# A gated linear-attention block with a squared-ReLU layer: units of 64 tokens of two batches, on quarters of the array

## The chip, the core and the metric

The kernel runs on one core of a Trainium2 chip, as one launch. The core has a matrix engine (TensorE, PE in the rows; its weight loads are listed as PEld), a vector engine (VectorE, DVE), a scalar engine (ScalarE, ACT), GpSimd (POOL) and a sync engine (SP) from which most transfers are issued. Each engine works through its own list of instructions in order. The metric is the device time of one execution in microseconds; lower is better.

## What is computed

Four batches, eight heads, 768 tokens, 48 channels a head, all in float32. For each batch and head a 48x48 state is carried from token to token; its output is reshaped to 384 channels and goes through a second layer that mixes each token with the one before it:

```
cur   = (u * k_t) v_t^T
y_t   = r_t (state + cur)
state = w * state + k_t v_t^T

xk = mu_k * x + (1 - mu_k) * x_prev          (x: y of all heads, 384 wide)
xr = mu_r * x + (1 - mu_r) * x_prev
out = sigmoid(xr @ w_r) * (relu(xk @ w_k)^2 @ w_v)     (d_ff = 1024)
```

The term with `u` is called the bonus: it only weighs a token's own key and value.

## The kernel before

**Attention.** The recurrence is done in chunks: 128 tokens of one batch, all eight heads, six chunks a batch, 24 in all, walked batch by batch. `load` brings r and k with channels on the partitions (48 channels of an even head on partitions 0 to 47, of an odd head on 64 to 111), and from the ninth chunk on also r and k with tokens on the partitions (`nat`). `prepare` multiplies r and k with tables of powers of the decay (L206, VectorE) and builds the bonus: for the first eight chunks with small matmuls and transposes (L215, L221), later on GpSimd (L231, L232) with a VectorE reduction (L234); ScalarE then writes it on the diagonal of a 128x128 block per head (L240). `scores` (L250) multiplies keys with receptances, 128x128 tokens a head, and VectorE copies the causal part over the diagonal block (L253). `update` (L283) adds keys times values to the state, `outputs` multiplies state with receptance (L302) and values with scores (L307) into one accumulator, and `turn` (L323) copies the result to `xt`, whose last 16 rows of each half are filled by transfers (L329).

**Feed-forward.** A tile is 512 tokens in a row of one batch (or the end of one and the start of the next). `mix` makes the two mixtures, each split in a high and a low part; `ffn` does 8 blocks of keys, 3 of gates and 3 of values. Every product is three matmuls of 512 columns (high x high, high x low, low x high; L341): 72 + 27 + 72 = 171 a tile, 1026 in all. The weights arrive as 64-bit numbers in ten blocks, and each is turned into a high and a low part by ScalarE and VectorE (`split_weights`, L188 to L197: an absolute value, a clamp, a shift, two joins, a cast and a difference).

**Order.** Four chunks run ahead of the first tile. After that one step of the attention generator is put between feed-forward groups at a higher priority, and a scheduler settles the order on each engine. Idle matmuls (L98) fill the start.

The lines that the prediction touches: L206 (scaling), L240 and L253 (diagonal and mask), L229 to L234 (GpSimd's part), L250, L302, L307 and L283 (attention matmuls), L341 (feed-forward), L188 to L197 (weights).

Of the kernel before, what the change touches and what calls it, by code (L numbers as in the profile page):

```python
# [8 lines left out]
F32 = mybir.dt.float32  # L9
# [7 lines left out]
P = 128  # L17
B, H, S, D = 4, 8, 768, 48
C = 128
NC = S // C  # L20
# [9 lines left out]
TT = 512  # L30
TC = TT // C
NM = B * S // TT
# [5 lines left out]
BUSY, BUSY_LATER, BUSY_UPDATE, BUSY_COLS = 48, 24, 8, 192  # L38


AHEAD, PACE, URGENT = 4, 1.3, 1000

EARLY = 8

W_MIN, W_MAX = 0.75, 1.25

LEAST = 1.125 * 2.0 ** -15
G = P // (B * H)
# [3 lines left out]

def first_run(m):

    return min(TT, S - m * TT % S)


def runs(m, x):

    n = first_run(m)  # L60
    if n == TT:
        return x[:, 1:TT + 1], x[:, :TT]
    assert 2 * n == TT
    x = x[:, :TT + 2].rearrange("p (a n) -> p a n", a=2)
    return x[:, :, 1:], x[:, :, :n]
# [10 lines left out]
def rwkv_kernel(ctx, tc, rkT, nat, w_pair, u, u_pair, mu, r_seq, k_seq, v_seq, w_rep, u_rep, wk, wv, wr, out):  # L76
# [3 lines left out]
    inp = main.enter_context(tc.tile_pool(name="inp", bufs=2))  # L80
    att = main.enter_context(tc.tile_pool(name="att", bufs=2))
    xp = main.enter_context(tc.tile_pool(name="xp", bufs=2))
    moe = main.enter_context(tc.tile_pool(name="moe", bufs=2))
    stage = main.enter_context(tc.tile_pool(name="stage", bufs=2))
    psA = main.enter_context(tc.tile_pool(name="psA", bufs=2, space=bass.MemoryType.PSUM))
    psY = main.enter_context(tc.tile_pool(name="psY", bufs=3, space=bass.MemoryType.PSUM))
    psM = main.enter_context(tc.tile_pool(name="psM", bufs=3, space=bass.MemoryType.PSUM))

    idle = const.tile([P, BUSY_COLS], BF16, name="idle")
    nc.vector.memset(idle, 0.0)
    idle_ps = psM.tile([P, BUSY_COLS], F32, tag="m", name="idle_ps")

    def stay_busy(n, behind=None):
        with tc.issue_after(behind.ins) if behind else ExitStack():
            for _ in range(n):
                nc.tensor.matmul(out=idle_ps, lhsT=idle[:, :P], rhs=idle, start=True, stop=True, skip_group_check=True)  # L98

    stay_busy(BUSY)  # L100

    w_sb = const.tile([DR, NP], F32, name="w_sb")
    nc.sync.dma_start(out=w_sb, in_=w_pair)
    tiles = {}
    order = [(b, c) for b in range(B) for c in range(NC)]

    def load(b, c):
        rk = inp.tile([DR, 2, NP, C], F32, tag="rk", name=f"rk_{b}_{c}")  # L110
        nc.sync.dma_start(out=rk, in_=rkT[b, c])
        na = None
        if order.index((b, c)) >= EARLY:
            na = stage.tile([P, 2, DM], F32, tag="raw", bufs=2, name=f"nat_{b}_{c}")
            nc.sync.dma_start(out=na, in_=nat[b, c, :, :2])
        v = inp.tile([P, DM], F32, tag="v", bufs=3, name=f"v_{b}_{c}")
        nc.sync.dma_start(out=v, in_=nat[b, c, :, 2])
        tiles[b, c] = rk, na, v

    load(0, 0)  # L120
    u_sb = const.tile([DR, NP, 2], F32, name="u_sb")
    nc.sync.dma_start(out=u_sb, in_=u_pair)
    ident = const.tile([P, P], F32, name="ident")
    make_identity(nc, ident)
    causal_f = const.tile([P, C], F32, name="causal_f")
    nc.gpsimd.memset(causal_f, 1.0)
    nc.gpsimd.affine_select(out=causal_f, in_=causal_f, compare_op=ALU.is_gt, fill=0.0,
                            base=0, pattern=[[1, C]], channel_multiplier=-1)
    causal = causal_f.bitcast(U32)
    S_t = []  # L130
    for i in range(2):
        t = const.tile([DR, NP, HB], F32, name=f"S_{i}")
        nc.gpsimd.memset(t, 0.0)
        S_t.append(t)

    w_in = const.tile([DR, NP], F32, name="w_in")
    nc.vector.tensor_scalar(out=w_in, in0=w_sb, scalar1=W_MIN, scalar2=W_MAX, op0=ALU.max, op1=ALU.min)
    zero = const.tile([DR, 1], F32, name="zero")
    nc.vector.memset(zero, 0.0)
    zero = zero.broadcast_to([DR, C])  # L140

    table = const.tile([DR, 2, NP, C + 1], F32, name="table")
    pw, ipw = table[:, 0], table[:, 1, :, :C]
    nc.vector.memset(pw[:, :, 0:1], 1.0)
    for p in range(NP):
        nc.vector.tensor_tensor_scan(
            out=pw[:, p, 1:], data0=w_in[:, p:p + 1].broadcast_to([DR, C]), data1=zero,
            initial=1.0, op0=ALU.mult, op1=ALU.add)
    last_inv = const.tile([DR, NP, 1], F32, name="last_inv")
    nc.vector.reciprocal(out=last_inv, in_=pw[:, :, C:])  # L150
    nc.vector.tensor_tensor(out=ipw, in0=pw[:, :, C - 1::-1], in1=last_inv.broadcast_to([DR, NP, C]), op=ALU.mult)
    mu_sb = const.tile([P, 2, CT], F32, name="mu_sb")
# [442 lines left out]
```

## Time and profile before

| | |
|---|---|
| median of 2 runs | 406.65 us (405.02 and 408.28) |
| profiled execution, first to last instruction (span) | 408.4 us |
| TensorE busy | 394.9 us, 97% of the span |
| VectorE, ScalarE, GpSimd busy | 219.0, 235.6, 69.4 us |
| mean granted TensorE clock | 0.914 of full speed |
| last matmul ends, span ends | 401.9 us, 408.4 us |

One execution is profiled. Busy time adds up the durations of an engine's instructions where they do not overlap; a matmul that waits in the pipeline counts as busy, so TensorE at 97% is not TensorE at its peak. The chain of waits starts at the last instruction and follows back what released each step. The granted clock has two levels here, 1.2 and 2.4 GHz, given as 0.50 and 1.00; a figure between them is a mean over a stretch. A float32 matmul of the program appears as two TensorE instructions, so counts of attention matmuls in the rows are twice those of the program; the feed-forward ones appear once.

### The profile page before, as it was taken

To read this page: it belongs to the slowest core of one execution; us is meant where nothing else is said; L and a number is where in the kernel's file an instruction comes from. 1 tells how busy PE (TensorE), PEld (TensorE's weight loads), DVE (VectorE), ACT (ScalarE), POOL (GpSimd) and SP (SyncE) were. 2 spreads that over 40 slices of the span, in tenths; PEclk is the share of its full clock that TensorE was granted. 3 is DMA by queue.
4 is the path that set the end of the run, shared out by engine and by line. 5 is a ranking of instruction groups with operands and counts; after the bars stand their busy time and mean duration, and the time that the engine had idled before them with its cause. 6 is when DMAs were issued, how large, how long until landed. Compare 5 with 4: busy or idle time off the path is not lost.

```text
span 408.4 us, 6780 instructions
## 1 busy us (share of the span) xinstructions
PE 394.9 (97%) x2660; PEld 319.7 (78%) x2660; DVE 219.0 (54%) x338; ACT 235.6 (58%) x489; POOL 69.4 (17%) x66
## 2 busy tenths in 40 slices
PE   8999979998999999999999999999999999999993
PEld 7888867886678877677878887878888888888882
DVE  6569959986365854436782467641255136213110
ACT  3644647769855549764660988750894189128400
POOL 1000000068064503234630181000000000000000
PEclk9555985579999999997799999999999999999999
DMA  7646575432166131244442430001000100010001
GB/s 226 192 137 201 142 221 151 153 121 79 39 169 182 45 124 58 85 126 136 130 130 69 130 119 24 2 28 46 26 2 26 51 2 0 26 54 0 2 35 50
DMA packets 15463, 36.11 MB, mean 88 GB/s; under 512 B 2560, under 2 KB 7296, under 8 KB 15424
## 3 DMA queue, kind: packets, MB, share of 16 engines
q1 hardware_dynamic: 15424, 35.60, 28.3%
q8 instruction: 23, 0.38, 0.4%
q14 instruction: 16, 0.13, 0.1%
HBM read 29.70 MB, written 4.72 MB: 84 GB/s over the span
## 4 chain that ended last, share of the span: by engine, by line
PE 85%; DMA 4%; POOL 3%; DVE 3%; ACT 2%; issue 1%; POOLq 0%; DVEq 0%; ACTq 0%; SPq 0%
PE v L341 25%; PE k L341 22%; PE r L341 10%; PE a L250 9%; PE y L307 6%; PE y L302 6%; PE kt_ps L215 2%; DMA raw_v<-in_wv 2%; DMA nat<-in_nat 2%; PE idle_ps L98 2%; PE u L283 1%; POOL ku L231 1%; PE kt_ps L221 1%; ACT am L240 1%; PE u L273 1%
## 5 line engine op out<-in xcount | busy, mean ns | idle before, releaser
L372 ACT ACTIVATE kr<-k 128x512 f32<-128x512 f32 x48 | 28.5, 597 | 61.1 <-PE k L341 56.3
L377 DVE TENSOR_TENSOR kl<-kr,kh 128x512 fp32r<-128x512 f32 x48 | 35.1, 733 | 50.1 <-ACT kh L375 49.8
L341 PE MATMUL k<-xh,wk_hi 128*128 128x512 f32 x144 | 57.9, 405 | 1.4 <-ACT kr L372 1.4
L341 PE MATMUL k<-xl,wk_hi 128*128 128x512 f32 x144 | 57.2, 397 | 0.0
L341 PE MATMUL v<-kl,wv_hi 128*128 128x512 f32 x144 | 56.8, 395 | 0.0
L341 PE MATMUL v<-kh,wv_lo 128*128 128x512 f32 x144 | 56.6, 393 | 0.0
L341 PE MATMUL k<-xh,wk_lo 128*128 128x512 f32 x144 | 56.5, 392 | 0.0
L341 PE MATMUL v<-kh,wv_hi 128*128 128x512 f32 x144 | 56.4, 392 | 0.0
L240 ACT ACTIVATE am<-ident,dg 128x128 f32<-128x128 f32 x128 | 39.9, 390 | 24.2 <-PE y L307 13.4
L250 PEld LDWEIGHTS a<-RK 48*128 48x128 f32 x384 | 39.3, 221 | 9.5 <-issue 7.3
L250 PE MATMUL a<-RK 48*128 48x128 f32 x384 | 46.6, 323 | 0.0
L253 DVE COPY_PREDICATED am<-causal_f,a 128x512 f32<-128x512 uint32 x48 | 34.1, 730 | 18.9 <-PE a L250 13.7
L391 DVE TENSOR_TENSOR sg<-v,sg 128x512 f32<-128x512 f32 x18 | 12.4, 689 | 58.8 <-PE v L341 58.8
L231 POOL TENSOR_TENSOR ku<-nat,u_bc 128x384 f32<-128x384 f32 x16 | 24.3, 1516 | 106.6 <-DMA nat<-in_nat 98.0
L206 DVE TENSOR_TENSOR RK<-rk,table 112x1024 f32<-112x1024 f32 x24 | 30.2, 1256 | 13.6 <-PE y L302 9.0
L307 PE MATMUL y<-am,v 128*48 128x128 f32 x384 | 36.2, 319 | 0.4 <-DVE am L253 0.3
L302 PE MATMUL y<-RK,S 48*48 48x128 f32 (+1 forms) x320 | 32.1, 311 | 2.8 <-ACT kt L224 2.8
L341 PEld LDWEIGHTS k<-xh,wk_hi 128*128 128x128 f32 x144 | 27.3, 190 | 8.7 <-ACT kr L372 1.8
L341 PEld LDWEIGHTS v<-kh,wv_lo 128*128 128x128 f32 x144 | 27.0, 188 | 6.5 <-issue 0.4
L341 PEld LDWEIGHTS k<-xh,wk_lo 128*128 128x128 f32 x144 | 27.2, 189 | 6.1 <-issue 0.2
L341 PEld LDWEIGHTS v<-kh,wv_hi 128*128 128x128 f32 x144 | 27.0, 188 | 6.0
L341 PEld LDWEIGHTS v<-kl,wv_hi 128*128 128x128 f32 x144 | 27.1, 188 | 5.8
(94 smaller groups left out, 612.7 us busy)
## 6 DMA issues: line engine op xcount, KB each, us to landing
rk<-in_rkT SPq DMA_DIRECT2D x24, 448.0 KB, 4.0
nat<-in_nat SPq DMA_DIRECT2D x16, 384.0 KB, 3.3
v<-in_nat SPq DMA_DIRECT2D x24, 192.0 KB, 3.7
raw_k<-in_wk SPq DMA_DIRECT2D x4, 768.0 KB, 5.8
raw_v<-in_wv SPq DMA_DIRECT2D x4, 768.0 KB, 4.3
out<-sg SPq DMA_DIRECT2D x12, 256.0 KB, 2.0
out<-sg SPq DMA_DIRECT2D x12, 128.0 KB, 1.8
raw_r<-in_wr SPq DMA_DIRECT2D x2, 576.0 KB, 3.7
```

Source lines behind the costliest of these rows:

```text
L98: nc.tensor.matmul(out=idle_ps, lhsT=idle[:, :P], rhs=idle, start=True, stop=True, skip_group_check=True)
L206: nc.vector.tensor_tensor(out=RK, in0=rk, in1=table[:, :, :, :C], op=ALU.mult)
L231: nc.gpsimd.tensor_tensor(out=ku, in0=na[:, 1], in1=u_bc, op=ALU.mult)
L240: nc.scalar.mul(out=am[:, p], in_=ident, mul=dg[:, 2 * p + s:2 * p + s + 1])
L250: mm = nc.tensor.matmul(out=a_ps[s][:, p, :], lhsT=K[rows, p, :], rhs=R[rows, p, :], start=True, stop=True, skip_group_check=True)
L253: nc.vector.copy_predicated(out=Am[s], mask=causal.unsqueeze(1).broadcast_to([P, NP, C]), data=a_ps[s])
L302: nc.tensor.matmul(out=y_ps[s * HB:s * HB + n, p, :], lhsT=state[b, c][rows, p, :n], rhs=R[rows, p, :], start=(p == 0), stop=False, skip_g ...
L307: nc.tensor.matmul(out=y_ps[s * HB:s * HB + D, p, :], lhsT=v[:, h * D:(h + 1) * D], rhs=Am[s][:, p, :], start=(c == 0 and p == 0), stop=(p ...
L341: nc.tensor.matmul(out=ps, lhsT=a, rhs=x, start=(i == 0), stop=(i == n - 1))
L372: nc.scalar.activation(out=kr, in_=k_ps, func=AF.Relu)
L377: nc.vector.tensor_tensor(out=kl, in0=kr, in1=kh.bitcast(F32), op=ALU.subtract)
L391: nc.vector.tensor_tensor(out=sg[o], in0=v_ps, in1=sg[o], op=ALU.mult)
```

## The change

**Units.** A unit is 64 tokens of two batches, all eight heads; there are 12 x 2 = 24 units, again each a 24th of the work, and two units cover the same 64 tokens of all four batches. Partition halves now hold the two batches (for tokens) or two heads (for channels), so that each matmul uses one quarter of the array, 64 rows by 64 columns, and four consecutive ones use four different quarters. A unit has 80 small matmuls in the program: 16 for the bonus (`L250`, two columns each), 16 scores of 64 columns (`L256`), 16 from the state (`L287`), 16 with the values (`L300`), 16 for the update (`L318`, 48 columns). The last three go into one accumulator of two banks. Because state and value matmuls write the same cells from different rows, the value matmuls wait for a one-element GpSimd write (`tick`) that itself waits for the last state matmul.

**Other engines.** The diagonal is one VectorE product (L264) instead of eight ScalarE ones; the bonus product `ru`, the scaled keys `Kn` and the decayed state `dec` are GpSimd's; the loads of r in token order are gone. Of each weight block GpSimd does the clamp, and for the last six blocks also the low part.

**Tiles and order.** A tile is 128 tokens of all four batches, again 512 columns. The first tile's keys are done in two halves of 256 columns, the first after units 0 and 1 alone. The order is written out by hand: a start, then four units per tile at fixed steps (2, 5, 8 and 11 of 23) with the next tile's gap transfers at step 12 and its mixing after that. Loads run three units ahead.

```
+    def scale(u, engine=None):
+        d["ru"] = ru = sb.tile([DR, 2 * NP, C], F32, tag="ru", bufs=1, name=f"ru_{u}")
+        nc.gpsimd.tensor_tensor(out=ru, in0=d["rk"][:, 0], in1=d["rk"][:, 1], op=ALU.mult)
+        (engine or nc.vector).tensor_tensor(out=RK, in0=d["rk"], in1=table[:, :, :, :C], op=ALU.mult)
...
+    def scores(u):
...
+        for p in range(NP):
+            for r in range(2):
+                for z in range(2):
+                    nc.tensor.matmul(out=a[z * C:(z + 1) * C, r, p * C:(p + 1) * C], lhsT=key(K, r, z, p),
+                                     rhs=key(R, r, z, p), start=False, stop=(p == NP - 1), skip_group_check=True)
...
+    def mask(u):
...
+        nc.vector.tensor_tensor(out=Am, in0=id64.unsqueeze(1).unsqueeze(1).broadcast_to([P, 2, NP, C]),
+                                in1=dg.broadcast_to([P, 2, NP, C]), op=ALU.mult)
+        nc.vector.copy_predicated(out=Am, mask=causal.unsqueeze(1).unsqueeze(1).broadcast_to([P, 2, NP, C]),
+                                  data=a[:, :, :NP * C].rearrange("a r (p t) -> a r p t", p=NP))
...
+    def from_state(u):
...
+        for p in range(NP):
+            for r in range(2):
+                for z in range(2):
+                    s = r ^ z
+                    n = (HB, D)[s]
+                    mm = nc.tensor.matmul(out=d["y"][s * HB:s * HB + n, z, p * C:(p + 1) * C],
+                                     lhsT=S_t[q][r * HB:r * HB + D, z, p, :n], rhs=key(R, r, z, p),
+                                     start=(p == 0), stop=False, skip_group_check=True)
+        d["tick"] = nc.gpsimd.memset(tick, 0.0)
+        behind_of(d["tick"], mm)
...
+    def block(u, then=None):
+        new_y(u)
+        from_state(u)
+        if u + 1 < NU:
+            scores(u + 1)
+        elif then:
+            then()
+        values(u)
+        update(u)
+    def behind(u):
+        if u + 1 < NU:
+            mask(u + 1)
+        turn(u)
+        advance(u)
+        if u + 2 < NU:
+            scale(u + 2)
+            decayed(u + 2)
+        if u + 1 < NU:
+            scale_k(u + 1)
+        if u + 3 < NU:
+            load_rk(u + 3)
+            load_v(u + 3)
+            load_k(u + 3)
...
+    for f in range(FT):
+        kk[f] = new_keys(0, f, sb, TT)
+        keys_of("0a", f, parts[0], TT // 2, sb, psM, first, kk[f])
+        if f == 1:
+            block(2)
+            behind(2)
+            w_join(2)
+            load_w(4)
+            w_rest(2, nc.vector)
+            w_clamp(3)
+        if f == 3:
+            block(3)
+            behind(3)
+            fill_gaps(0, 1 + C, 1 + L, (nc.sync, nc.scalar))
...
```

The order on TensorE, in the middle of the program. Before, one feed-forward matmul stands between pieces of a chunk (`a` are scores, `y` outputs, `r` gates):

```order
L307 MATMUL y_5_1664<-am_5_0_1516,v_5_1388 48x128
L341 MATMUL r_1_1640<-xh_0_1_1153,wr_hi 128x512
L302 MATMUL y_1_2005<-RK_1_1777,S_149 64x128
L250 MATMUL a_2_0_1976<-RK_2_1927 128x128
L250 MATMUL a_2_1_1977<-RK_2_1927 128x128
```

In the change, from the last state matmuls of unit 8 to its first value matmuls (`a` are the scores of the unit after):

```order
L287 MATMUL y_1717<-RK_1389,S_108 48x64 x2
L287 MATMUL y_1717<-RK_1389,S_108 64x64
L250 MATMUL a_1735<-u_sb,ru_1527 64x2 x16
L256 MATMUL a_1735<-RK_1529 64x64 x16
L300 MATMUL y_1717<-Am_1522,v_1240 64x64 x2
L300 MATMUL y_1717<-Am_1522,v_1240 48x64 x2
```

The score and bonus matmuls of the next unit now stand between a unit's state and value matmuls, in one piece, and no feed-forward matmul stands among them.

The order on GpSimd. Before, from the middle of the program (`ku` is the bonus product, `dec` the decayed state):

```order
L231 TENSOR_TENSOR ku_4_2169<-nat_4_2042,u_bc 128x384
L232 TENSOR_TENSOR ku_4_2169<-ku_4_2169,nat_4_2042 128x384
L229 TENSOR_TENSOR Kn_3_2048<-nat_3_1923,wn 128x384
L279 TENSOR_TENSOR dec_1_1947<-S_149,table 112x192
L279 TENSOR_TENSOR dec_2_2066<-S_151,table 112x192
L229 TENSOR_TENSOR Kn_4_2167<-nat_4_2042,wn 128x384
L279 TENSOR_TENSOR dec_3_2185<-S_149,table 112x192
```

In the change, up to the second and the third of the ticks, those of units 3 and 4 (`a_v` is a weight block being clamped, `wv_lo` its low part; numbers in names are the scheduler's):

```order
L241 TENSOR_TENSOR Kn_810<-kn_524,wn 128x400
L233 TENSOR_TENSOR ru_804<-rk_666 112x512
L326 TENSOR_TENSOR dec_662<-S_108,table 112x384
L204 TENSOR_SCALAR a_v_1417<-a_v_1417 128x768
L290 MEMSET tick 1x1
L233 TENSOR_TENSOR ru_1073<-rk_812 112x512
L223 TENSOR_TENSOR wv_lo<-a_v_1278,wv_hi 128x768
L223 TENSOR_TENSOR wv_lo<-a_v_1417,wv_hi 128x768
L241 TENSOR_TENSOR Kn_1079<-kn_670,wn 128x400
L326 TENSOR_TENSOR dec_808<-S_109,table 112x384
L233 TENSOR_TENSOR ru_1230<-rk_1081 112x512
L290 MEMSET tick 1x1
```

The ticks, which TensorE waits for, stand behind weight clamps and low parts that the program before had on VectorE.

The order on VectorE, near the start, beginning with the scaling of the third chunk. Before:

```order
L206 TENSOR_TENSOR RK_2_292<-rk_2_213,table 112x1024
L212 TENSOR_TENSOR ru_2_294<-rk_2_213 112x512
L189 TENSOR_SCALAR a_k_363<-a_k_363 128x768
L192 SCALAR_TENSOR_TENSOR a_k_280<-raw_k_278,a_k_280 128x768
L253 COPY_PREDICATED am_1_0_232<-causal_f,a_1_0_252 128x512
L318 MEMSET xt_788 128x4
L253 COPY_PREDICATED am_1_1_237<-causal_f,a_1_1_253 128x512
```

In the change, where `RK_361` is the scaling of unit 2 and `Am_304` the diagonal and mask of unit 1:

```order
L216 SCALAR_TENSOR_TENSOR a_k_241<-early_75,a_k_241 128x768
L235 TENSOR_TENSOR RK_361<-rk_239,table 112x1024
L223 TENSOR_TENSOR wk_lo<-a_k_241,wk_hi 128x768
L212 TENSOR_SCALAR a_k_354<-a_k_354 128x768
L214 SCALAR_TENSOR_TENSOR a_k_354<-early_75,a_k_354 128x768
L216 SCALAR_TENSOR_TENSOR a_k_354<-early_75,a_k_354 128x768
L264 TENSOR_TENSOR Am_304<-id_95,a_270 128x512
L266 COPY_PREDICATED Am_304<-causal_f,a_270 128x512
L223 TENSOR_TENSOR wk_lo<-a_k_354,wk_hi 128x768
```

The mask of unit 1, on which the first tile's first half rests, stands behind the scaling of unit 2 and the joins of the second weight block.

## Rows read from the trace of the kernel before

**Rows 1.** The page: TensorE's busy time and instructions.

```profile
PE 394.9 (97%) x2660; PEld 319.7 (78%) x2660; DVE 219.0 (54%) x338; ACT 235.6 (58%) x489; POOL 69.4 (17%) x66
```

**Rows 2.** Windows: length, each engine's busy us (x instructions), clock, DMA.

```profile
0.00:65.60 65.60, 60.50 (x521) 52.95 (x521) 48.72 (x86) 33.97 (x75) 1.59 (x10) 0.71 0.59 179
65.60:94.20 28.60, 27.14 (x165) 21.87 (x164) 24.89 (x36) 21.61 (x51) 8.59 (x6) 0.64 0.48 156
...
250.00:402.00 152.00, 151.83 (x720) 123.86 (x718) 53.17 (x81) 78.96 (x134) 0.00 (x0) 1.00 0.06 21
```

**Rows 3.** Chain of waits, late: start us, us, what.

```profile
284.41 16.48 PE k L341 x72
300.89 6.18 PE r L341 x27
...
401.92 0.69 DVE sg L391
```

**Rows 4.** Chain of waits, attention matmuls at the full clock.

```profile
124.58 0.36 PE u L283 x16
...
153.65 0.49 PE u L283 x16
...
254.58 1.10 PE a L250 x16
255.68 1.01 PE y L302 x15
256.69 1.01 PE y L307 x16
```

**Rows 5.** Chain of waits, a stretch in which TensorE waited.

```profile
230.34 4.19 DMA nat<-in_nat
...
238.06 2.15 POOL dec L279
```

**Rows 6.** Timeline of DVE, start: start us, us, instruction [idle before].

```profile
5.53 1.22 DVE L206 TENSOR_TENSOR RK<-rk,table 112x1024 f32<-112x1024 f32 x1
...
17.55 1.23 DVE L206 TENSOR_TENSOR RK<-rk,table 112x1024 f32<-112x1024 f32 x1 [3.44 <-DMA rk<-in_rkT]
```

**Rows 7.** Groups of DVE: count, busy us, mean ns of one, idle.

```profile
L253 DVE COPY_PREDICATED am<-causal_f,a 128x512 f32<-128x512 uint32 x48 | 34.1, 730 | 18.9 <-PE a L250 13.7 <-ACT am L240 4.7 <-issue 0.2
L206 DVE TENSOR_TENSOR RK<-rk,table 112x1024 f32<-112x1024 f32 x24 | 30.2, 1256 | 13.6 <-PE y L302 9.0 <-DMA rk<-in_rkT 4.6
...
L361 DVE TENSOR_TENSOR xl<-xm,xh 128x512 fp32r<-128x512 f32 x36 | 25.2, 709 | 8.0 <-ACT xh L359 7.8
...
L192 DVE SCALAR_TENSOR_TENSOR a_k<-raw_k,a_k 128x768 uint32<-128x768 uint32 x4 | 3.8, 954 | 0.1
...
L197 DVE TENSOR_TENSOR wk_lo<-a_k,wk_hi 128x768 fp32r<-128x768 f32 x4 | 3.8, 950 | 0.1
...
L190 DVE TENSOR_SCALAR a_k<-a_k 128x768 uint32<-128x768 uint32 x4 | 2.2, 553 | 0.0
```

**Rows 8.** Timeline of POOL, beside a busy and an idle DVE.

```profile
85.53 3.81 POOL L231 TENSOR_TENSOR ku<-nat,u_bc 128x384 f32<-128x384 f32 x1 [83.30 <-DMA nat<-in_nat]
...
236.70 1.00 POOL L229 TENSOR_TENSOR Kn<-nat,wn 128x384 f32<-128x384 f32 x1
...
242.09 0.51 POOL L279 TENSOR_TENSOR dec<-S,table 112x192 f32<-112x192 f32 x1
```

**Rows 9.** Timeline of DVE beside POOL.

```profile
87.78 0.68 DVE L361 TENSOR_TENSOR xl<-xm,xh 128x512 fp32r<-128x512 f32 x1
...
90.94 1.29 DVE L197 TENSOR_TENSOR wv_lo<-a_v,wv_hi 128x768 fp32r<-128x768 f32 x1
```

**Rows 10.** Timeline of TensorE, two matmul streams on different columns.

```profile
83.64 0.31 PE L273 MATMUL u<-v,kt 128*48 128x48 f32 x1
83.64 0.45 PE L307 MATMUL y<-am,v 128*48 128x128 f32 x1
```

**Rows 11.** DMA issues: transfer, count, KB each, us to landing.

```profile
xt<-xt SPq DMA_DIRECT2D x24, 32.0 KB, 2.0
```

More of the change, by code (lines that the diff above doesn't have):

```diff
@@ L18 @@
 B, H, S, D = 4, 8, 768, 48
-C = 128
-NC = S // C
 NP = H // 2
@@ L50 @@
 TB = 16
[L53 to L65, printed above, removed]
+IDLE_COLS = 192
 def channels(t):
@@ L100, in rwkv_kernel @@
[L100 to L118, printed above, removed]
@@ L247, in scores, with values @@
+    def values(u):
+        j, q = order[u]
+        d = units[u]
         for p in range(NP):
             for s in range(2):
[L249 to L253 removed]
@@ new lines, in update @@
+    def update(u, alone=False):
+        j, q = order[u]
+        d = units[u]
+        if j == NJ - 1:
+            return
+        if alone:
+            new_y(u)
+        for p in range(NP):
+            for r in range(2):
+                for z in range(2):
+                    h, n, rows = 2 * p + (r ^ z), (HB, D)[r], slice(z * C, (z + 1) * C)
+                    at = NP * C + p * D
+                    nc.tensor.matmul(out=d["y"][r * HB:r * HB + n, z, at:at + D],
+                                     lhsT=d["Kn"][rows, h * D:h * D + n], rhs=d["v"][rows, h * D:(h + 1) * D],
+                                     start=(alone and p == 0), stop=(p == NP - 1), skip_group_check=True)
@@ L337, in matmul3, with weight @@
+    def weight(name, i, j):
+        n = FT if name == "v" else CT
+        return [w.rearrange("p i n -> p (i n)")[:, (i * n + j) * P:(i * n + j + 1) * P] for w in W[name]]
+    def matmul3(ps, pairs, first=True, last=True):
         n = 3 * len(pairs)
@@ new lines, in rwkv_kernel @@
+    load_rk(2)
+    w_clamp(0)
+    late_tables()
+    new_y(0)
+    values(0)
+    scores(1)
+    turn(0)
+    mask(1)
+    load_k(0)
+    load_v(2)
+    load_w(2)
+    stay_busy(10)
+    new_y(1)
+    values(1)
+    turn(1)
+    load_rk(3)
+    load_k(1)
+    fill_gaps(0, 1, 1 + C, (nc.sync, nc.scalar))
+    w_join(0)
+    w_clamp(1)
+    scale_k(0)
+    scale(2)
+    w_rest(0, nc.vector)
+    scores(2)
+    stay_busy(10)
+    update(0, True)
+    advance(0)
+    load_v(3)
+    load_k(2)
+    load_w(3)
@@ new lines, in rwkv_kernel @@
+    scale_k(1)
+    update(1, True)
+    advance(1)
+    mask(2)
+    load_rk(4)
+    load_v(4)
+    load_k(3)
+    stay_busy(20)
+    parts = new_parts(0, sb, TT)
+    for _ in mix_tile(0, parts, 0, C, (0,)):
+        pass
+    decayed(2)
+    decayed(3)
+    scale(3)
+    scale_k(2)
+    w_join(1)
+    w_rest(1, nc.vector)
+    w_clamp(2)
+    load_k(4)
+    stay_busy(10)
+    kk = {}
+    first, second = (lambda x: halves(x, 0, C)), (lambda x: halves(x, C, L))
+    for f in range(FT):
[12 more added lines that the diff above has]
+            fill_gaps(0, 1 + C, 1 + L, (nc.sync, nc.scalar))
+            load_w(5)
+            w_join(3)
+            w_rest(3, nc.vector)
+            w_clamp(4)
```

676 lines of the change are left out of this document (353 added, 323 removed).

## The prediction

> **What bounds the kernel now.** The page first: TensorE is busy 394.9 us, 97% of the span [rows 1], so the question is which of these are at full speed. The windows tell [rows 2]. From 250 to 402 us it is busy 151.83 of 152 us at clock 1.00, while VectorE has 53.17 us of work: this stretch is TensorE alone. In the first 65.6 us it is "busy" 60.5 us but at clock 0.71, and to 94.2 us at 0.64, with VectorE at work for 48.72 and 24.89 us: here TensorE is filled with slow or idle work, and attention and weight preparation on the other engines set the pace. The chain of waits prices TensorE's full speed: 72 feed-forward matmuls take 16.48 us, so 0.2289 us each, and from the last of them to the end of the span pass 408.4 - 401.92 = 6.5 us [rows 3]. A chunk costs 1.10 us for scores, 1.01 for the state part, 1.01 for the values, and 0.36 for the update, 0.49 where feed-forward work follows it [rows 4]; 3.6 us in all.
>
> So 1026 x 0.2289 = 234.9 us of feed-forward, 24 x 3.6 = 86 us of attention and 6.5 us of tail make 327.4 us. The other 81 us are the slow start and a few stretches of waiting, such as a 4.19 us transfer of `nat` and a 2.15 us `dec` on GpSimd in the chain between 230 and 246 us [rows 5]. The change can win in the start, in such stretches, and in the price of a chunk. I rebuild the time as four terms: until TensorE becomes the bound, feed-forward after that, attention after that, and tail.
>
> **Term 1, the start: 84 us.** The order shows where TensorE becomes the bound: with the second half of the first tile's keys (`k_0b`), behind the value matmuls of unit 4. VectorE must by then have scaled seven units (1.26 us each), joined eight weight blocks (0.55 + 0.95 + 0.95 = 2.45 each) and two of three quarters that size (1.84), made four low parts (0.95), six diagonals and masks (two of 0.73 each, taking the diagonal like the copy) and the first key mixtures and key remainders, ten passes of 512 columns together (0.71 each), plus four state writes, about 0.7 each [rows 7]: 8.8 + 19.6 + 3.7 + 3.8 + 8.8 + 7.1 + 2.8 = 54.6 us. It can begin at about 5.5 us, when the first scaling starts today [rows 6]. The third unit's load will be late as the third chunk's is now, 3.44 us of idle before the scaling at 17.55 [rows 6], and more by a further weight block ahead of it; the mask of unit 1 and all that follows stands behind it. With that wait and the gap transfers of unit 3 (2.0 us each [rows 11]), 68 us if nothing interferes.
>
> GpSimd interferes. It must deliver, before the tick of unit 4: eight `ru` of 512 columns, six `Kn` of 400, four `dec` of 384, two low parts of 576 and four of 768 columns, and ten clamps. Undisturbed, 384 columns with two inputs take 1.00 us and 192 take 0.51 [rows 8], hence 10.6 + 6.2 + 4.1 + 3.0 + 8.0 = 31.9 us. A clamp on GpSimd is in no row: 768 columns take 0.55 us on VectorE [rows 7] and by GpSimd's rate 2.0 us with two inputs [rows 8]; with one input I take 1.3, so 12.4 us (bounds 5 to 19). In all 44 us. And the two engines exclude each other: beside a VectorE that is working without pause, a product of 1.00 us took 3.81 [rows 8], while VectorE's own instruction kept its 0.68; where GpSimd was first, a 0.95 us low part took 1.29 [rows 9]. Masks and state writes read the accumulator and were not stretched. If everything else excludes, 5.5 + (54.6 - 8.8 - 2.8) + 44 = 93 us. Some of GpSimd's work falls under masks and VectorE's waits, some 12 to 15 us. Between 68 and 93 I take 84, nearer to the upper end, because a full exclusion is what these rows show [rows 8, 9]. TensorE's own work in that time (72 keys of 256 columns, four units) is 25 us at full clock and fits even at half.
>
> **Term 2, feed-forward after the start: 227 us.** 954 matmuls of 512 columns x 0.2289 = 218.4. The 72 of 256 columns lie between 0.114 (half) and 0.229 each; the columns decide, so 0.12, or 8.6 us (8.2 to 16.5).
>
> **Term 3, attention after the start: 54 us.** Units 5 to 23 hold 19 state, 36 score and bonus, 19 value and 17.5 update groups, 91.5 groups of 16 small matmuls (32 instructions). No row shows four quarters at once. Today 16 instructions of 128 columns take 1.01 us in eight pairs [rows 4], 0.126 us a pair; at 64 columns 0.063 a set. Eight sets of four are 0.50 us, the lower bound. The update of today, 48 columns, runs at 0.36/16 = 0.0225 us an instruction; if that were the pace at which they can be issued, a group is 0.72 us. I take 0.53, near the first, since 0.045 a pair of 48 columns is itself about 48/128 of 0.126. A change between quarter and full work costs 0.49 - 0.36 = 0.13 [rows 4], 0.3 a unit with both ends. 91.5 x 0.53 + 19 x 0.3 = 54.2 (51 to 72). A unit is 3.0 us after 3.6: the bonus comes back to TensorE and eats most of what the smaller scores save.
>
> **What lies beside it.** The tick makes the value matmuls wait, with update and feed-forward queued behind; the score and bonus matmuls, 1.06 us by the price above, stand between, and after the start GpSimd has 1.33 + 1.04 + 1.02 = 3.4 us of work in the 9 us between units. The diagonal's 39.9 + 19.6 us leave ScalarE, which was not the bound late. Per unit VectorE has 1.46 + 1.26 + 0.7 us, which fits. The six gap transfers (2.0 us) and the mixing of a tile, six times about 1.5, stand ahead of 72 feed-forward matmuls or 16.5 us of cover; if the cover went, 2 to 4 us a tile would show. For waits at unit and tile edges and the clock's return I add 4 us (bounds 0, as from 250 to 402 us, and 16, the whole stretch from 230 to 246 us [rows 5]). Loads lose `nat` of 384 KB and are issued three units ahead.
>
> **Sum.** 84 + 227 + 54 + 4 + 6.5 = 375.5 us against the profiled span of 408.4. The median of the two runs, 406.65, is 1.7 us under that span, so **374 us**. This measurement can tell about 2% from no change: faster is below 398.5, slower above 414.8.
>
> **The rivals.** *The start is shorter.* GpSimd's work falls into VectorE's waits and the start is 68 us: 358 us. For it: GpSimd stretched to 3.81 without slowing VectorE [rows 8, 9]. Against: VectorE waits for its clamps. Chance 0.15.
>
> *The start is longer.* With clamps of 2.0 us and masks that exclude too, 100 us or more: 390 to 399. For it: the ticks stand behind weight work. Chance 0.15, two thirds of it still faster by 2%.
>
> *A pace of issue.* Two matmuls on different columns start within 0.01 us of each other [rows 10], but over sixteen the closest mean is 0.0225 us [rows 4]. If instructions can't follow faster than that, or up to a tenth slower with four quarters in turn, a group is 0.72 to 0.80 us: 374 + 91.5 x 0.19 to 0.27 = 391 to 399 us, about half of it no change. Chance 0.10. The Trainium skill, "TensorE: Matmul & The Clock Gate", section "Wait — 56ns, not 53.3ns?", states that starts of matmuls never come closer than about 25 ns however few their columns; by it a group would be 32 x 0.025 = 0.80 us and the time 399. The closest mean here lies slightly under it [rows 4].
>
> *Slower: quarters run two at a time.* All pairs that run at once today are two row halves, two column halves or a diagonal. If four are served as two and two, a group is 16 x 0.063 = 1.01 us: 374 + 91.5 x 0.48 = 418 us. It decides from (414.8 - 374)/91.5 + 0.53 = 0.98 us a group. Against it: scores pair rows and values pair columns, both near 1 us a group [rows 4]. Chance, with worse forms and mixtures, 0.09.
>
> The forecast itself has 0.51 (362 to 390). That the change does not do what it says is excluded by the order on TensorE. The range 352 to 404 holds the forecast, both starts and the issue pace. Faster: 0.51 + 0.15 + 0.10 and half of the issue rival, 0.05, with a point off for mixtures, 0.80; slower 0.09; within 2% the rest, 0.11.
>
> **What would show it.** In the changed kernel: the first `k_0b` near 84 us, VectorE and GpSimd each busy over 70% before it, and GpSimd's products there well over their undisturbed 1.3 and 1.0 us. A group of sixteen (L256, L287, L300) at 0.5 to 0.6 us in the chain, L250 the same although it has two columns. From the start to the last matmul a clock of 1.00 and TensorE busy all but 4 us. I am wrong if L256 takes 0.8 us or more, if `k_0b` starts outside 66 to 100 us, or if value matmuls wait for the tick in every unit.

## The result, and the profile after

The changed kernel takes 385.14 us (two runs, 384.99 and 385.29) beside 406.65 us. The ratio on record is 0.950, 95% interval 0.934 to 0.967 (the quotient of these two medians is 0.947). Ratios leave out executions of the kernel before in a slower state, which beside the last four experiments are those from 407.85 us up. The change is faster, inside the range of 352 to 404 and 11 us above the forecast of 374. The span of its profiled execution is 383.3 us where the sum of terms said 375.5. The first part of its page answers to [rows 1]: engine, busy time, share of the span, instructions.

```profile
PE 334.7 (87%) x4926; PEld 280.4 (73%) x4926; DVE 239.5 (62%) x307; ACT 181.1 (47%) x311; POOL 113.0 (29%) x119
PEclk9965567657979999999999999999999999999998
```

TensorE is busy 60 us less and ScalarE 54; GpSimd and VectorE are busy longer. The clock row (40 slices of 9.6 us, tenths of full speed) is low from the third slice to the twelfth (but for the eleventh). So the span is cut at the first receptance matmul, at 107.65 us, behind which TensorE is the bound. The windows' columns are the stretch, its length, busy time and instructions of each engine, granted clock, share of DMA, GB/s:

```profile
0.00:107.65 107.65, 66.55 (x1378) 61.40 (x1379) 89.08 (x120) 47.19 (x94) 57.92 (x59) 0.73 0.49 151
...
107.65:376.90 269.25, 268.11 (x3549) 219.00 (x3548) 149.71 (x187) 133.88 (x217) 55.08 (x60) 0.99 0.22 66
```

Ahead of the mark TensorE is at work for 67 of 108 us at clock 0.73 and VectorE for 89; behind it TensorE for all but 1.1 of 269 us. The late chain of waits (start, length, what) prices what happens there, as [rows 3, 4] did before:

```profile
207.66 0.59 PE y L287 x29
208.25 0.45 PE a L250 x29
208.70 0.52 PE a L256 x32
209.22 0.45 PE y L300 x31
209.67 0.47 PE y L318 x28
210.14 2.28 PE r L392 x9
...
337.15 16.73 PE k L392 x72
...
376.98 0.69 DVE sg L428
```

A unit is 2.48 us from state to update. The nine receptance matmuls behind it take 2.28 us, 0.19 more than nine at 0.232, so a unit is 2.67 with its switches, where a chunk was 3.6 us [rows 4]. A feed-forward matmul costs slightly more than it did (16.73/72 = 0.232 us beside 0.229), which is about 3 us over the 954 behind the mark. The tail is 6.3 us.

The kernel before has the same mark, its first receptance matmul. There too the first tile's keys are done and the values of seven chunks, as here of seven units. Its row in the timeline, and the window from there to its last matmul:

```profile
106.60 0.50 PE L341 MATMUL r<-xh,wr_hi 128*128 128x512 f32 x1
...
106.60:401.90 295.30, 294.81 (x1921) 235.59 (x1920) 137.13 (x208) 168.57 (x345) 52.74 (x45) 0.98 0.21 64
```

So the change gains nothing ahead of the mark (107.65 beside 106.60 us), and all of the 25.1 us between the two profiled spans behind it: 269.25 us in place of 295.30. Seventeen units at 3.6 - 2.67 us are about 16 of these 26 us. The rest is time that the kernel before spends over its chain's price of a chunk, with the pieces of a chunk scattered between feed-forward matmuls; how it divides no run shows.

Up to the mark TensorE waits for 41 us of the 107.65. In its timeline (start, length, engine, line, operation, the idle time before it and what ended that) groups whose x32 stands in one row are whole:

```profile
73.01 0.68 PE L250 MATMUL a<-u_sb,ru 48*64 48x2 f32 x32 [2.01 <-DVE Am L266]
...
81.40 1.03 PE L250 MATMUL a<-u_sb,ru 48*64 48x2 f32 x32 [5.09 <-DVE Am L266]
82.25 1.13 PE L287 MATMUL y<-RK,S 48*64 48x64 f32 x32
85.93 1.12 PE L300 MATMUL y<-Am,v 64*64 64x64 f32 x32 [2.54 <-POOL tick L290]
86.84 0.39 PE L318 MATMUL y<-v,Kn 64*64 64x48 f32 x2
87.16 0.79 PE L392 MATMUL k_0b<-xh,wk_hi 128*128 128x256 f32 x2
```

TensorE stands before masks (`Am`) and a tick. VectorE meanwhile works on value weights, which nothing needs before 111 us, and some of its passes are stretched (0.96 us is what the join of 2.44 us takes at 78.94, and 1.23 what the scaling of 3.10 us takes alone [rows 6]):

```profile
57.65 0.94 DVE L216 SCALAR_TENSOR_TENSOR a_v<-raw_v,a_v 128x768 uint32<-128x768 uint32 x1
...
60.30 2.44 DVE L216 SCALAR_TENSOR_TENSOR a_v<-raw_v,a_v 128x768 uint32<-128x768 uint32 x1
...
67.63 3.10 DVE L235 TENSOR_TENSOR RK<-rk,table 112x1024 f32<-112x1024 f32 x1
...
78.94 0.96 DVE L216 SCALAR_TENSOR_TENSOR a_v<-raw_v,a_v 128x768 uint32<-128x768 uint32 x1
79.81 0.68 DVE L264 TENSOR_TENSOR Am<-id,a 128x512 f32<-128x512 f32 x1
80.53 0.73 DVE L266 COPY_PREDICATED Am<-causal_f,a 128x512 f32<-128x512 uint32 x1
```

Two questions follow: what makes a group of sixteen as cheap as 0.45 to 0.59 us, and what sets the first 108 us.

### The profile page after: what moved, and what is told of

The parts are those of the page before. It is cut to its first block, busy times and chain, and to the rows that moved or that the text cites. A ratio compares the mean times of both kernels' runs of the same rounds, so it can differ in the third digit from the quotient of the medians.

```text
span 383.3 us, 11167 instructions
## 1 busy us (share of the span) xinstructions
PE 334.7 (87%) x4926; PEld 280.4 (73%) x4926; DVE 239.5 (62%) x307; ACT 181.1 (47%) x311; POOL 113.0 (29%) x119
## 4 chain that ended last, share of the span: by engine, by line
PE 71%; DVE 11%; DMA 6%; issue 5%; ACT 3%; POOL 2%; ACTq 1%; DVEq 0%; POOLq 0%; SPq 0%
PE v L392 26%; PE k L392 22%; PE r L392 11%; PE y L287 3%; DMA early<-in_wk 2%; PE a L256 2%; PE y L300 2%; PE y L318 2%; PE a L250 2%; DMA kn<-in_k 2%; DVE RK L235 2%; DVE a_v L216 1%; POOL Kn L241 1%; DMA raw_v<-in_wv 1%; DVE kl L417 1%
## 5 line engine op out<-in xcount | busy, mean ns | idle before, releaser
L417 DVE TENSOR_TENSOR kl<-kr,kh 128x512 fp32r<-128x512 f32 x40 | 49.7, 1242 | 42.7 <-ACT kh L416 42.0
L392 PE MATMUL k<-xh,wk_hi 128*128 128x512 f32 x120 | 48.3, 403 | 0.0
L398 DVE SCALAR_TENSOR_TENSOR xm<-xt,mu_sb,xm 128x512 f32<-128x512 f32 (+1 forms) x39 | 27.3, 710 | 33.4 <-ACT xm L397 32.6
L392 PE MATMUL k<-xl,wk_hi 128*128 128x512 f32 x120 | 47.3, 394 | 0.0
L233 POOL TENSOR_TENSOR ru<-rk 112x512 f32<-112x512 f32 x24 | 41.5, 1729 | 9.7 <-PE a L250 5.1
L397 ACT ACTIVATE xm<-xt,omu 128x512 f32<-128x512 f32 (+1 forms) x39 | 26.3, 689 | 30.0 <-DMA xt<-xt 27.5
L344 ACT COPY xt<-y 112x512 f32<-112x512 f32 x24 | 14.2, 590 | 38.3 <-PE y L318 29.9
L241 POOL TENSOR_TENSOR Kn<-kn,wn 128x400 f32<-128x400 f32 x22 | 27.1, 1233 | 14.2 <-PE y L318 10.5
L300 PE MATMUL y<-Am,v 64*64 64x64 f32 (+1 forms) x768 | 18.1, 234 | 13.2 <-ACT wk_hi L218 10.3
L401 DVE TENSOR_TENSOR xl<-xm,xh 128x512 fp32r<-128x512 f32 (+1 forms) x39 | 26.6, 688 | 2.1 <-ACT xh L400 1.3
## 6 DMA issues: line engine op xcount, KB each, us to landing
early<-in_wk SPq DMA_DIRECT2D x3, 768.0 KB, 11.9
```

Of the source, the lines that this page charges most:

```text
L233: nc.gpsimd.tensor_tensor(out=ru, in0=d["rk"][:, 0], in1=d["rk"][:, 1], op=ALU.mult)
L241: nc.gpsimd.tensor_tensor(out=Kn, in0=d["kn"], in1=wn, op=ALU.mult)
L300: mm = nc.tensor.matmul(out=d["y"][s * HB:s * HB + n, z, p * C:(p + 1) * C], lhsT=d["v"][rows, h * D:h * D + n], rhs=d["Am"][rows, s ^ z, ...
L344: nc.scalar.copy(out=xts[m][:DR, :, 2 * q:2 * q + 2, c0:c0 + C].rearrange("a p z t -> a z p t"), in_=y)
L392: nc.tensor.matmul(out=ps, lhsT=a, rhs=x, start=(first and i == 0), stop=(last and i == n - 1))
L397: nc.scalar.mul(out=xm, in_=before, mul=omu[:, j, t:t + 1])
```

## The experiments

All kernels start from the changed one. The first two lots of four have no run of the changed kernel beside them, so there differences under 3 us mean little; the last four have one (382.97 us). The stages of each profiled run:

| kernel | first `k_0b` | first receptance matmul | from there to the last matmul (TensorE idle in it) | median |
|---|---|---|---|---|
| before | none | 106.6 | 295.3 (0.5) | 406.65 |
| changed kernel | 87.2 | 107.7 | 269.2 (1.1) | 385.1 |
| the same again | 86.6 | 107.4 | 269.3 (1.0) | 383.0 |
| one_quarter | 86.9 | 116.8 | 329.4 (0.0) | 455.5 |
| two_quarters | 86.4 | 109.1 | 279.4 (0.3) | 395.8 |
| split_scores | 87.1 | 112.9 | 281.0 (5.4) | 401.6 |
| no_bonus_matmuls | 69.1 | 92.6 | 268.3 (2.3) | 369.1 |
| weights_on_vector | 82.5 | 107.5 | 268.7 (1.8) | 382.5 |
| whole_first_keys | none | 107.7 | 270.7 (2.1) | 384.2 |
| late_value_weights | 70.6 | 95.2 | 278.8 (7.6) | 382.9 |
| late_on_vector | 68.7 | 98.0 | 274.6 (5.0) | 380.0 |
| spread_gpsimd | 71.0 | 94.5 | 270.1 (0.9) | 373.2 |
| spread_values | 69.0 | 98.6 | 272.3 (3.6) | 379.5 |
| spread_joined | 69.9 | 93.8 | 276.9 (2.4) | 376.9 |

Behind the mark all have the same feed-forward work, and all kernels made from the changed one have the same units (no_bonus_matmuls one more).

### What a group of small matmuls costs

**One quarter at a time, and two.** In all five groups the loops over row half `r` and column half `z` go outside:

```
-        for p in range(NP):
-            for r in range(2):
-                for z in range(2):
+        for r in range(2):              # two_quarters: r, p, z
+            for z in range(2):
+                for p in range(NP):
```

> The same small matmuls, but the four quarters no longer take turns: all of one quarter, then all of the next. Theory (a group of sixteen takes 0.45 to 0.59 us because four quarters work at once, 0.063 us for each of eight sets): now sixteen times two instructions follow one another on their quarter, 32 x 0.063 = 2.0 us a group, +1.5 us for the 91.5 groups behind the start, about 137 us: 385 + 137 = 522 us, a little less if neighbours at the edge of two quarters overlap. Rival (a pace of issue or something else that doesn't ask for quarters sets the group's price): the same 385 us, groups of 0.45 to 0.6 us.

> The same small matmuls, but only the two quarters of one row half take turns, then the two of the other. Theory (quarters at once set the price): 16 x 0.063 = 1.0 us a group, +0.5 us for 91.5 groups, 46 us: about 431 us. This is the price that the prediction's slower rival gave the change itself. Rival (not the number of quarters, but the number of instructions sets it): 385 us.

Measured 455.5 and 395.8 us: both slower than the changed kernel, and both far less than expected. In two_quarters the expectation describes bonus, scores and state alone: there two column halves of one row half take turns. In values and update the same edit leaves two row halves of one column half in turn. The order of the quarters sets the price, but 0.063 us for an instruction is wrong. The timeline of one_quarter behind 216 us shows it: 26 bonus instructions of two columns from 218.20 to about 219.1, and the score instructions of 64 columns at the same pace.

```profile
216.90 1.32 PE L287 MATMUL y<-RK,S 48*64 48x64 f32 x29
...
218.20 1.03 PE L250 MATMUL a<-u_sb,ru 48*64 48x2 f32 x26
...
219.27 1.14 PE L256 MATMUL a<-RK 48*64 48x64 f32 x26
...
220.42 1.69 PE L300 MATMUL y<-Am,v 64*64 64x64 f32 x26
```

In two_quarters a unit's chain runs from 212.80 to 216.01, 3.2 us in place of 2.48, not 5.

```profile
212.80 0.73 PE y L287 x23
...
213.70 0.34 PE a L250 x20
...
214.21 0.44 PE a L256 x20
...
214.83 0.56 PE y L300 x23
...
215.55 0.47 PE y L318 x24
216.01 1.13 PE r L392 x4
```

**Same columns, more instructions.**

```
-  nc.tensor.matmul(out=a[z * C:(z + 1) * C, r, p * C:(p + 1) * C], ... rhs=key(R, r, z, p), ...)
+  for t in range(0, C, C // 2):
+      nc.tensor.matmul(out=a[..., r, p * C + t:p * C + t + C // 2], ...
+                       rhs=key(R, r, z, p)[:, t:t + C // 2], ...)
```

> Each score matmul is made as two of 32 columns in place of one of 64: the same columns, twice the instructions. As the prediction worked the group's price out (columns decide: eight sets of four quarters, 0.063 us each at 64 columns), a score group stays near 0.50 us and the time at 385 us. If each instruction has its own price whatever its columns, as the bonus group with 2 columns at 0.45 us and the runs with fewer quarters suggest, the group goes to 0.95 us, 19 groups behind the start make 8.6 us, 394 us.

Measured 401.6 us. Its timeline has the group with 64 instructions beside groups with 32:

```profile
208.37 0.62 PE L250 MATMUL a<-u_sb,ru 48*64 48x2 f32 x32
208.83 1.15 PE L257 MATMUL a<-RK 48*64 48x32 f32 x63
209.76 0.25 PE L302 MATMUL y<-Am,v 64*64 64x64 f32 x1
```

From 208.83 to 209.76 are 0.93 us where 64 columns in half as many instructions took 0.52. With four quarters in turn the instruction is the unit of price, as the second reading said. (The rest of the 16 us is not the group: 5 us lie ahead of the mark, 4.3 us are new idle time behind it.)

**Half the bonus instructions, over all rows.** On spread_values (below), one matmul takes both row halves:

```
-  for r in range(2): ... lhsT=key(d["ru"], r, z, p), rhs=key(u_sb, r, z, p)
+  lhsT=d["ru"][:, z * NP + p], rhs=u_both[:, z * NP + p]    # 112 rows; a column of u per row half
```

> spread_values with the bonus of both row halves made by one matmul over all 112 rows: 8 bonus matmuls a unit in place of 16, the same result. If each instruction has its price (14 ns with four quarters in turn, 15 to 22 with two), a unit's bonus takes 0.22 to 0.35 us in place of 0.44, and 24 units gain 2 to 5 us over spread_values. If the columns or the ways through the array decide, or if leaving the quarters costs a switch of 0.13 us at both ends, nothing is gained, or 2 us are lost.

Measured 376.9 us, 2.6 us under spread_values, but not for that reason: behind the mark it is 4.6 us longer. What makes up for that lies ahead of the mark (93.8 beside 98.6 us), where its lists are in another order; the two profiled executions differ by only 0.3 us in span. The price went as the second reading had it:

```profile
207.80 0.69 PE L297 MATMUL y<-RK,S 48*64 48x64 f32 x32
208.43 0.63 PE L259 MATMUL a<-u_both,ru 112*64 112x2 f32 x16
208.99 0.69 PE L265 MATMUL a<-RK 48*64 48x64 f32 x32
209.51 0.64 PE L310 MATMUL y<-Am,v 64*64 64x64 f32 x32
```

Sixteen instructions over 112 rows take 0.56 us, thirty-two on quarters 0.44, and the state group ahead of them grows to 0.63. Together, as the time from one instruction's start to the next one's, over all groups of a line behind the mark (512 or 544 instructions, 256 in spread_joined's bonus):

| ns an instruction | bonus, 2 columns | scores, 64 | state, 64 | values, 64 |
|---|---|---|---|---|
| four quarters in turn | 13.7 | 15.4 | 15.6 | 14.7 |
| scores of 32 columns | 14.5 | 14.7 | 15.6 | 15.8 |
| two halves in turn (columns; in values rows) | 15.4 | 21.5 | 22.2 | 22.9 |
| one quarter | 35.1 | 36.6 | 37.6 | 40.9 |
| bonus over 112 rows | 35.2 | 16.1 | 19.5 | 14.7 |

Columns hardly count with four quarters in turn, or with one. With two halves in turn they do: 15.4 ns for 2 columns, 21.5 to 22.9 for 64. Which halves take turns makes little difference there. Nor does the accumulator's bank: in two_quarters it stays the same in a row half's scores and changes from one state matmul to the next, and the two cost 21.5 and 22.2. Each instruction has a weight load of its own in the traces (behind the mark 512 loads beside 512 score instructions, and 1024 beside 1024 in split_scores, where neighbours have the same weights). So the price is that of an instruction with its load, and no run takes the two apart.

### What sets the start

**Clamps and low parts to VectorE.**

```
-        nc.gpsimd.tensor_scalar(out=a..., scalar1=MOST, scalar2=LEAST, ...)
+        nc.vector.tensor_scalar(out=a..., scalar1=MOST, scalar2=LEAST, ...)
...
-    w_rest(b, nc.gpsimd)
+    w_rest(b, nc.vector)
```

> The clamps and the last six low parts of the weight blocks move from GpSimd to VectorE; nothing else is changed. Theory (the two engines exclude each other in the start, so what counts is the sum of their work): ten clamps of about 0.83 us and six low parts of about 1.8 us leave GpSimd (19 us), about 11 us come to VectorE (0.55 and 0.95 us each). The sum falls by 8 us, so the second half of the first tile's keys starts 3 to 8 us before the 87.2 us of the changed kernel, and the time is 377 to 382 us. Rival (VectorE's own list sets the start, GpSimd's work is hidden beside it): VectorE's list grows by 11 us, the keys start near 98 us, the time is about 396 us.

Measured 382.5 us. The keys start 4.6 us sooner, as the theory had it, although VectorE's list is longer; but the first receptance matmul comes at 107.5 us as before. The rival's 396 us fell outright. Nineteen us off GpSimd pay for eleven on VectorE and no more.

**Value weights held back.** A block's join waits for the latest feed-forward matmul written ahead of it:

```
+        first = nc.vector.tensor_scalar(out=a, in0=a, scalar1=3, ...)
+        if name == "v":
+            behind_of(first, latest[0])
...
+        latest[0] = mm              # behind each group of feed-forward matmuls
```

> The joins of the four value-weight blocks, which nothing needs before the first value projection, are held until keys of the second half (two of them until later projections) have been issued; no work is added or left out. In the changed kernel their twelve VectorE passes take 12.1 us between 55 and 80 us, among the masks and state writes of units 3 to 5, and GpSimd's four low parts 7.8 us between 59 and 83 us. Theory (the start is set by VectorE's list in its order, stretched by GpSimd): the first keys of the second half come 8 to 15 us before 87.2 us, the stretch from there to the first receptance matmul (20.5 us) grows by up to 5 us, the time is 373 to 379 us. Rival (loads and the chain of a unit through mask, values and state set the start, VectorE's weight passes fill its waits): the keys start near 87 us, the time is 385 us, or longer if the values' weights come too late.

Measured 382.9 us, and it fits neither reading whole. The first keys of the second half start at 70.6 us, 16.6 us sooner, and the mark comes at 95.2 us, 12.4 us sooner: value-weight work in the lists ahead of masks and state writes did set much of the start. It is work of two engines. With VectorE's twelve passes, GpSimd's four low parts (7.8 us) move behind those keys; up to them VectorE is busy 17.2 us less and GpSimd 10.1, and this run does not tell which counts. But 7.6 us of idle time stand behind the mark. The timeline names a chain on three engines, once ahead of the mark and once behind it, and another wait for a tick:

```profile
88.70 0.89 ACT L203 ACTIVATE a_v<-raw_v 128x768 f32<-128x768 f32 x1 [1.99 <-DMA raw_v<-in_wv]
89.49 0.58 ACT L348 COPY xt<-y 112x512 f32<-112x512 f32 x1
...
90.17 0.56 DVE L341 TENSOR_TENSOR S<-y,dec 112x384 f32<-112x384 f32 x1 [2.52 <-ACT xt L348]
...
90.78 1.13 PE L291 MATMUL y<-RK,S 48*64 48x64 f32 x32 [4.61 <-DVE S L341]
...
100.95 0.89 ACT L203 ACTIVATE a_v<-raw_v 128x768 f32<-128x768 f32 x1 [3.91 <-DMA raw_v<-in_wv]
...
103.03 1.13 PE L291 MATMUL y<-RK,S 48*64 48x64 f32 x32 [2.46 <-DVE S L341]
...
107.61 2.18 POOL L227 TENSOR_TENSOR wv_lo<-a_v,wv_hi 128x768 fp32r<-128x768 f32 x1 [1.76 <-ACT wv_hi L222]
109.87 1.11 PE L304 MATMUL y<-Am,v 64*64 64x64 f32 x32 [4.00 <-POOL tick L294]
```

ScalarE waits in its list for a weight block, whose load waited for a buffer; the copy of a unit's output stands behind it, then VectorE's state write, then TensorE. This chain is 2.46 of the 7.6 us behind the mark. The larger wait there, 4.00 us, is for a tick that stands behind a low part on GpSimd, and the expectation of spread_gpsimd below doesn't name it.

> The same hold, and clamps and low parts on VectorE as in weights_on_vector. If what counts is the sum of VectorE's and GpSimd's work ahead of the second half's keys, this lowers it once more, by about 5 us: 370 to 376 us. If VectorE's own list counts, moving 11 us of work to it costs some of what the hold gives: 380 us or more.

Measured 380.0 us, where the second reading begins. Beside late_value_weights the mark is 2.8 us later and the idle time behind it 2.6 us shorter, and no wait for a tick is left there. Both ran on the same chip, and the runs lie at 378.6 to 381.2 us here and at 380.8 to 383.7 there: nineteen us of GpSimd for eleven of VectorE cost nothing here and gained 2.9 us in the medians.

**The first tile's keys whole**, not in two halves (in outline):

```
-    for f in range(FT): keys_of("0a", f, ...) ... units 2 and 3 in between
+    units 2 and 3, then
+            kk[f] = keys_of(m, f, parts[0], TT, sb, psM)
```

> The keys of the first tile are made whole, 72 matmuls of 512 columns behind unit 4, not half of them behind unit 1 and half behind unit 4. Theory (the first half's matmuls lie in TensorE's waits of the start and cost nothing): 72 x 0.229 in place of 72 x 0.119 us come behind the start, 7.9 us more; VectorE loses six passes or so of 0.4 to 0.5 us and eight key remainders of 0.42 from the start, at most 6 us: 387 to 393 us. Rival (VectorE's list alone sets the start): the start gets 6 us shorter and nearly pays for it, 385 to 387 us.

Measured 384.2 us, the rival's side, below its 385. The mark is where it was, 107.7 us: 8 us of feed-forward work taken out of the early waits were made up by a shorter list on VectorE. The early half keys bought nothing that can be measured.

**The bonus left out** (in outline).

```
-  the 16 matmuls of L250;  dg = a[:, :, NP * C:NP * C + 2 * NP]...
+  dg = no_bonus...            # a table of zeros
```

> The sixteen bonus matmuls of each unit are left out and the diagonal is taken from a table of zeros, so the bonus term is missing from the output; the product ru is still made on GpSimd. Theory (behind the start TensorE alone is the bound, so its price counts in full): 19 to 20 groups x 0.45 us = 8.8 us less, 376 us. Rival (the group's time lies beside something else that ends last): no change, 385 us.

Measured 369.1 us, 16 less. A unit behind the mark costs 2.16 us where it cost 2.52 (sums of the groups' means), so about 7 us over 19 units. The other 9 are not the bonus's price: without it the scheduler put three of the four value blocks behind the first keys of the second half, and the mark came at 92.6 us. That agrees with the hold above.

### A version that beats both

Two points of late_value_weights are moved: the steps at which blocks are joined, and ScalarE's pass of the last two, which is held too.

```
-   at in (2, 4, 7, 9, 11):   b = {2: 5, 4: 6, 7: 7, 9: 8, 11: 9}[at]
+   at in (2, 3, 6, 11, 14):  b = {2: 5, 3: 6, 6: 7, 11: 8, 14: 9}[at]
...
+   first = nc.scalar.activation(out=a..., func=AF.Abs)
+   if name == "v" and i > 1:
+       behind_of(first, latest[0])
```

> The changed kernel without an edit, beside the three below on the same chip, so that differences of one per cent can be read: 385 us.

> late_value_weights with two points moved. There the joins of the value weights gave 12 us of the start, but 7.6 us of waits came back behind it, and the trace shows the order of it: ScalarE's first pass of a block (an absolute value) waits for the block's load, which waits for a buffer that the join two blocks before still holds; behind that pass stands ScalarE's copy of a unit's output, behind that VectorE's state write, behind that TensorE. Now the first two joins come one key earlier each, the last two not before the value projection that runs while they are made, and ScalarE's pass of these two is held as well. If that chain is the cause, 4 to 7 of the 7.6 us go: 374 to 379 us. If instead VectorE simply has too much to do between 70 and 112 us, the waits stay: 382 us.

> spread_gpsimd with clamps and low parts on VectorE, as in late_on_vector. Less for GpSimd ahead of each tick, more for VectorE: if GpSimd's products in front of the tick are what remains, 2 to 4 us less than spread_gpsimd, 371 to 376 us; if VectorE's list is, 2 to 4 us more.

The changed kernel takes 382.97 us here, a ratio to before of 0.946 (0.939 to 0.953). spread_gpsimd takes 373.2 us, 0.923 (0.917 to 0.930): faster than both, and none of its six runs (371.9 to 375.5) reaches the changed kernel's (381.4 to 384.8). The idle time behind the mark is 0.9 us: neither the wait on the chain through ScalarE nor the one for the tick comes back there. The edit moves the joins and ScalarE's pass together, so it shows that their places in the lists were the cause, not which of the two. Its windows up to the mark:

```profile
0.00:94.50 94.50, 63.98 (x1379) 58.42 (x1379) 77.23 (x111) 43.64 (x91) 52.87 (x55) 0.76 0.56 165
```

VectorE has 77.2 us there in place of 89.1, which is 11.9 us less, and the start is 13.2 us shorter. spread_values takes 379.5 us: the same 11 us of weight work on VectorE that were a draw in weights_on_vector cost 6.3 us here, 4.1 of them ahead of the mark. With the value weights spread, VectorE's list is the dearer place for it; in late_on_vector, with other places for the joins, it was not.

## Why the prediction was right, and where it was not

**That it gets faster, and by what.** Right in the main: the largest part of the gain that the rows price is the unit, 2.67 us where a chunk was 3.6, about 16 of 26 us behind the mark. By the forecast's own terms the mark would have come at 84 + 8.6 us of keys + 6.2 of attention = 99 us, 8 us sooner than in the kernel before. It came at 107.65. That is the whole of the 7.8 us between 375.5 and 383.3: behind the mark the terms add up to 277 us with the tail, and 275.7 were measured.

**Term 3, attention behind the start (forecast 54, bounds 51 to 72).** The 81 groups behind the mark take 40.7 us, 0.50 each, where 0.53 was forecast, and the unit's 2.67 us stand beside 3.0. The number held and its reason fell. The forecast took columns as the price: 0.063 us for a set of four at 64 columns, out of pairs of 128 columns [rows 4]. Two columns cost 13.7 ns and 64 cost 15.4; on one quarter it is 35.1 and 36.6. What four quarters give is that instructions overlap, from 36 down to 15 ns, a factor of 2.4 and not 4. The step that failed is "at 64 columns 0.063 a set"; it came out near because 4 x 15 ns happens to be 0.06 us, which is luck. The forecast also gave the bonus, with two columns, the price of 64; that came true, but columns as the price would not give it.

**The rivals on that price.** Two at a time was priced at 1.01 us a group; two_quarters, which does just that, has 0.49 to 0.73. Even so the time would have been 396 us, not 418, so that rival could not have made the change slower than before. A pace of issue was the right kind of mechanism with the wrong figure: it is 0.014 us, not 0.0225, a pace which instructions of 48 columns in pairs had shown [rows 4]. The Trainium skill, "TensorE: Matmul & The Clock Gate", section "Wait — 56ns, not 53.3ns?", puts the closest starts at about 25 ns; 13.7 ns over 512 instructions disagrees with it, and the measurement decides. The Trainium skill, "TensorEngine Tiling (Array Packing)", section "Instruction Overhead", says that a matmul of one column takes as long as one of 60; the one_quarter row agrees with that, 35.1 beside 36.6 ns.

**Term 1, the start until `k_0b` (forecast 84).** Measured 87.2, but 84 was VectorE's list and GpSimd's added up with some overlap, and GpSimd was busy 58% of the first 80 us where over 70% was forecast. What showed in the runs: the order of the lists counts, not the sum of the work alone. The value weights' twelve passes on VectorE and four low parts on GpSimd, moved behind the second half's keys, gave 12.4 and 13.2 us of the mark; nineteen us taken off GpSimd for eleven on VectorE gave 4.6 us of `k_0b` and none of the mark. Clamps were dearer in the forecast (1.3 us, measured 0.83 undisturbed), and VectorE, said to keep its time beside a product of GpSimd [rows 8], was stretched too.

**Term 4, waits (forecast 4, bounds 0 to 16).** This is the term that was mis-sized, in the stretch from `k_0b` to the mark. TensorE was not the bound from `k_0b` on, as Term 1 had it. From 87.2 to 107.65 us it needed 8.6 us for keys and 5.6 for two units, 14.2, and took 20.5. It stood idle for 2.3 us of this, 1.04 of them until a mask came, and the mean granted clock was 0.83; from 87 to 90 us it was 0.50, where a 256-column matmul takes 0.213 us and not 0.119. With 1.6 us of receptance at half clock behind the mark and 1.1 of idle time that is 9 us, 5 over the forecast, and Term 1 was 3 over. Feed-forward was 3 us dearer than in Term 2, and Term 3 gave about 4 back. The prediction saw value weights only as work ahead of `k_0b`, not as work that could stand behind it.

**Term 2 and tail.** Right within 2%: 0.119 us for 256 columns at the full clock (forecast 0.12), 0.232 for 512, where 0.229 was taken over from the kernel before, and 6.3 us of tail (6.5). Value matmuls do not wait for the tick in every unit; behind the mark TensorE idles 1.1 us in all.

What stays open: why two column halves over 112 rows take 35 ns an instruction and over 48 rows 15; why a feed-forward matmul takes 0.232 us; and what part of the start is GpSimd's. Moving its weight work to VectorE was a draw at the mark with the value weights early, gained 2.9 us in the medians with them held, and lost 6.3 with them spread. No run leaves work out on one of the two engines alone.

## What to carry to other kernels

Price small matmuls by the instruction and by how their positions on the array follow one another, and look in the rows for two sizes at the same pace before scaling by columns. Where TensorE waits early, read the list of the engine it waits for: work that is ready but not needed yet, such as weights of a later stage, goes ahead of masks simply because it is ready, and a hold on it, with its places chosen by the waits that were left, was worth more here than any move to another engine. Whether a change gains in the start shows only when both kernels are read at the same amount of work done. When a wait is taken out, follow the next one to its first engine; it may be a load that a third engine waits for in its list.

## What the runs showed of the hardware

VectorE and GpSimd hold each other up in both directions. Around 200 us of the changed kernel, where nothing else is in the way:

```profile
199.40 1.23 DVE L235 TENSOR_TENSOR RK<-rk,table 112x1024 f32<-112x1024 f32 x1
200.69 2.62 DVE L417 TENSOR_TENSOR kl<-kr,kh 128x512 fp32r<-128x512 f32 x1
...
207.55 0.69 DVE L417 TENSOR_TENSOR kl<-kr,kh 128x512 fp32r<-128x512 f32 x1 [0.95 <-ACT kh L416]
```

```profile
199.92 1.84 POOL L233 TENSOR_TENSOR ru<-rk 112x512 f32<-112x512 f32 x1 [0.34 <-PE a L250]
201.72 1.04 POOL L241 TENSOR_TENSOR Kn<-kn,wn 128x400 f32<-128x400 f32 x1
```

`ru` (1.28 us alone, at 12.38) ends 1.13 us after the scaling does; the remainder `kl` (0.69 alone) is begun while `ru` runs, stands through `ru` and through `Kn` behind it, and ends 0.55 us after `Kn`. In [rows 8] it was GpSimd that stood; which of them stands depends on which came first, and two GpSimd instructions in a row leave VectorE no gap. The Trainium skill, "SBUF — State Buffer", section "SBUF: two separate sides", describes an exclusive lock that goes to the one that starts first; these rows agree. Over the whole run `kl` takes 1242 ns on the mean in the changed kernel and 690 in two_quarters. There it starts before the scaling has ended (205.20 us, the scaling ends at 205.28), `ru` had begun in the meantime, and it is `ru` that stands:

```profile
205.20 0.68 DVE L417 TENSOR_TENSOR kl<-kr,kh 128x512 fp32r<-128x512 f32 x1
204.67 2.35 POOL L233 TENSOR_TENSOR ru<-rk 112x512 f32<-112x512 f32 x1 [0.45 <-PE a L250]
```

`ru` ends 1.14 us after `kl`, as it ends 1.13 after the scaling in the changed kernel, where `kl` came 0.06 us after the scaling's end. As TensorE was the bound around 200 us of the changed kernel, the longer `kl` cost nothing there.
